# Attention with 32 heads: three independent pairs of probability tiles added by DMA, instead of three tiles added one after another into one sum

## The chip, the cores and the metric

The kernel runs on one core of a Trainium2 chip. The metric is the device time of one execution in microseconds (us). Before the change the median of three runs was 1824.03 us (1816.09, 1824.03, 1825.92).

## What is computed

For 2048 tokens of width 1024 the result is `g * a + (1 - g) * b`: `a` is softmax attention with 32 heads of width 32 and an output projection, `b` a small mixture of experts, `g` a sigmoid gate per token. The change lies in the attention, and there in the sums of the softmax rows:

```python
scores = einsum("bhqd,bhkd->bhqk", q, k) * (Dh ** -0.5)
p = softmax(scores, axis=-1)
o = einsum("bhqk,bhkd->bhqd", p, v)
a = o.transpose(0, 2, 1, 3).reshape(B, S, D) @ wo
```

The kernel takes exp(scores) without dividing, multiplies that with V, and divides by the row sums at the end. So it needs, per head and query, the sum of exp(scores) over the 2048 keys.

## The kernel before

**Tiles and steps.** A head has 16 tiles of 128 keys; its step k makes the tile `P[h, kt]`: 128 keys by 2048 queries, 1 MB in f32. The scores of a tile are four matmuls of 512 queries (L1284) into a ring of seven PSUM banks; ScalarE takes exp of one to four banks at once into the place of P (L1296); TensorE then multiplies P with V (L1308). A list of seven batches per head (L1527) writes the order of TensorE out by hand: 9, 9, 10, 9, 9, 9, 9 score matmuls, and behind those of each batch the products with V of the key tiles that are due (5, 5, 5, 4, 4, 5, 4 halves of a tile; the first five belong to the head before).

**Row sums.** `presum` (L1325) adds the 16 tiles of a head up. Twelve are added by VectorE into `acc` (`add`, L1339: two instructions of 1024 elements). Tile 1 is written by ScalarE straight into a buffer `accd`, and tiles 3, 8 and 12 are added to it by DMA (L1330: `nc.gpsimd.dma_start(ACCD[h], P[h, kt], accum_op=OP.add)`). All three write the same buffer, so each waits until the one before has landed. At step 3 of the next head VectorE adds `accd` to `acc` (`merge4`, L1372, for heads 0 to 23; `merge_even` and `merge_odd` after that; `merge` for the last two). Then DMAs of GpSimd's queue (`fold4`, L1381, and `fold4_end`, L1390) fold `acc` so that four heads (later two) share one tile T, which `head_sums` (L1395) sums over the partitions by matmuls with ones, at step 18 of the head after the fourth. `load_r` and `norm_r` (L1417, L1422) load the sums, take reciprocals and store them.

**Order of work.** Everything that is not a score or a V product is put at a step by `at(step, ...)` (L1470 to L1523), and each engine runs its own instructions in that order. DMAs of SP's queue (K, Q and V of the next head, stores) wait in order behind each other; so do those of GpSimd's queue (POOL in the profile: the accumulations and the folds).

**Places.** `p_tile` (L1158) gives a new tile the place whose planned end `until` is the earliest: 14 steps for a tile that DMA adds, 4 for another. There are 11 places, 9 from the 308th tile on and 8 from the 416th, when three of them (`vhl`, `wo_raw2`, `wo_raw3`) are wanted for weights. The two buffers of `accd` come on top. A place is free in fact when the V product, the addition or the DMA that reads it is done; ScalarE waits for that.

Of the kernel before, what the change touches and what calls it, by code (L numbers as in the profile page):

```python
# [10 lines left out]
F32 = mybir.dt.float32  # L11
# [21 lines left out]
def gated_mha_peer_kernel(ctx, tc, xT, wqkv, wv, wo, wq, k12, ug, v, out):  # L33
# [8 lines left out]
    nc = tc.nc  # L42
# [164 lines left out]
    pairs = [wa.tile([128, 2, 2, HC, 128], F32R, name=f"e{i}") for i in range(2)]  # L207
# [136 lines left out]
    places = {(2, 0): "xh2", (2, 1): "xl1", (3, 0): "xh3", (3, 1): "xl2"}  # L344
# [83 lines left out]
    second = {(0, 0): "A12", (0, 1): "A22", (1, 0): "S3", (1, 1): "S2"}  # L428
# [277 lines left out]
    for blk, (k, n) in enumerate(order):  # L706
        w, c = chunks[k]
        t = pairs[k % 2]
# [378 lines left out]
    def values_unit(u):  # L1087
# [11 lines left out]
        for k, name in enumerate(order):  # L1099
# [6 lines left out]
            if last and name == "P2":  # L1106
                first_scores()
# [39 lines left out]
                for j in {4: (0,), 5: (1,), 6: (2, 3)}.get(k, ()):  # L1147
                    split_early(u - 1, j)

    P, pools, keep = {}, {}, None  # L1150


    SUMS = (1, 3, 8, 12), (2, 4, 6)
    PLACES = (11, 0), (9, 28 * 11), (8, 28 * 11 + 12 * 9)
    LATE = 21, 28
    until = [0] * PLACES[0][0]

    def p_tile(h, kt):  # L1158


        n = [places for places, k in PLACES if pools["next"] >= k][-1]
        pools["next"] += 1
        i = min(range(n), key=lambda i: until[i])
        until[i] = h * NT + kt + (14 if kt in SUMS[h == H - 1] else 4)
        pool, name = ((pools["right"], f"P{i}") if i < 4 else (pools["left"], f"P{i}") if i < 8 else
                      (keep, ("vhl", "wo_raw2", "wo_raw3")[i - 8]))
        P[h, kt] = pool.tile([128, S], F32, name=name)
        return P[h, kt]

    def first_scores():  # L1170

        tp.close()
        pools.update(right=Pool("ppr", side="right"), next=0)
        K, Q = Z
        pt = p_tile(0, 0)
        for qc, i in enumerate((5, 6, 0, 1)):
            ps = ps1.tile([128, 512], F32, name=f"bk{i}")
            c = slice(qc * 512, (qc + 1) * 512)
            nc.tensor.matmul(ps, K[:98, :128], Q[:98, c], start=True, stop=True)
            nc.scalar.activation(pt[:, c], ps, AF.Exp, scale=SCALE)  # L1180
# [23 lines left out]
    keep = Pool("keep")  # L1204
# [4 lines left out]
    rb0 = keep.tile([128, KC, W], F32, name="rb0")  # L1209

    T = rb0.rearrange("p k m -> p (k m)")
# [5 lines left out]
    wk = Pool("wk", bufs=2)  # L1217

    ACC = {0: wk.tile([128, S], F32, name="acc")}
# [3 lines left out]
    pss = Pool("pss", space=PSUM)  # L1223

    KQ = [Z, [kq.tile([128, S], F32R, name=n) for n in ("K1", "Q1")]]
    Vt, O, SM, ACCD, R = {}, {}, {}, {}, {}


    NB = 7
# [41 lines left out]
    def scores(s0, s1):  # L1271


        n = s1 - s0
        banks = ring_banks(n)
        cuts = {c for c in range(1, n + 1) if c == n or (s0 + c) % NQ == 0 or banks[c] == 0}
        cuts |= set(range(1, max(1, n - NB) + 1))
        if n <= 2 * NQ:
            cuts |= {c + 2 for c in range(NQ, n, NQ) if not cuts & {c + 1, c + 3}}
        c0 = 0  # L1280
        for c, i in enumerate(banks):
            (h, kt), qc = divmod((s0 + c) // NQ, NT), (s0 + c) % NQ
            K, Q = KQ[h % 2]
            on_ring(nc.tensor.matmul(ring[:, i, :], K[:98, kt * 128:(kt + 1) * 128],  # L1284
                                     Q[:98, qc * 512:(qc + 1) * 512], start=True, stop=True), i)
            if c + 1 not in cuts:
                continue
            m = c + 1 - c0
            q0 = qc + 1 - m
            if q0 == 0:  # L1290
                if kt == SUMS[h == H - 1][0]:
                    P[h, kt] = ACCD[h] = wk.tile([128, S], F32, name="accd")
                else:
                    p_tile(h, kt)
            i -= m - 1
            on_ring(nc.scalar.activation(  # L1296
                P[h, kt][:, q0 * 512:(q0 + m) * 512].rearrange("p (a m) -> p a m", a=m),
                ring[:, i:i + m, :], AF.Exp, scale=SCALE), *range(i, i + m))
            c0 = c + 1
# [23 lines left out]
                                       start=(src is srcs[0]), stop=(src is srcs[-1]))  # L1323

    def presum(h, kt):  # L1325
        sums = SUMS[h == H - 1]
        if kt == 0 or kt == sums[0] or (h == H - 1 and kt >= NT - 2):
            return
        if kt in sums:
            nc.gpsimd.dma_start(ACCD[h], P[h, kt], accum_op=OP.add)  # L1330
            return
        if kt == 1 + (sums[0] == 1):
            if h > 0:
                ACC[h] = wk.tile([128, S], F32, name="acc")
            add(ACC[h], P[h, 0], P[h, kt])
        else:
            add(ACC[h], ACC[h], P[h, kt])

    def add(out, a, b):  # L1339

        for c in (slice(0, S // 2), slice(S // 2, S)):
            nc.vector.tensor_add(out[:, c], a[:, c], b[:, c])  # L1342

    def merge(h):
        add(ACC[h], ACC[h], ACCD[h])

    up, low = slice(0, 64), slice(64, 128)

    def merge_even(h):
        add(T, ACC.pop(h), ACCD[h])  # L1350

    def fold_even(h):
        nc.gpsimd.dma_start(T[up], T[low], accum_op=OP.add)

    def merge_odd(h):
        add(ACC[h][up], ACC[h][up], ACCD[h][up])
        add(T[low], ACC[h][low], ACCD[h][low])

    def fold_odd(h):
        nc.gpsimd.dma_start(T[low], ACC.pop(h)[up], accum_op=OP.add)  # L1360
# [3 lines left out]
    FOURS = 6  # L1364

    def quarter(i):
        return slice(32 * i, 32 * i + 32)
# [4 lines left out]
    def merge4(h):  # L1372
        q = h % 4
        if q == 0:
            add(T, ACC.pop(h), ACCD[h])
        else:
            mine = quarter(q)
            add(T[mine], ACC[h][mine], ACCD[h][mine])
            add(ACC[h], ACC[h], ACCD[h])

    def fold4(h):  # L1381
        q = h % 4
# [46 lines left out]
    OC, RB = {}, {}  # L1429
# [6 lines left out]

    def load_rb(n, k0, k1, js=range(4), queue=nc.sync):
        if k0 == 0 and js[0] == 0:
            RB[n] = rb0 if n == 0 else wk.tile([128, KC, W], F32, name="accd")
# [30 lines left out]
    def at(step, f, *a):  # L1470
        todo.setdefault(step, []).append((f, a))

    for h in range(H):
        base = h * NT
        g, j = divmod(h, 4)
        if h >= 1 and h + 1 < H:
            at(base - 1, load_head, h + 1)
        if h < H - 1:
            at(base + NT, finish, h)
            if h == H - 2:  # L1480
                at(base + NT + 5, merge, h)
                at(base + NT + 8, head_sums, h)
            elif g < FOURS:
                at(base + NT + 3, merge4, h)
                at(base + NT + 5, fold4, h)
                at(base + NT + 10, fold4_end, h)
            else:
                at(base + NT + 3, (merge_even, merge_odd)[h % 2], h)
                at(base + NT + 5, (fold_even, fold_odd)[h % 2], h)
                if h % 2:  # L1490
                    at(base + NT + 12, head_sums, h - 1, 2)
        if j == 3 and g + 1 < G:
            if g < FOURS:
                at(base + NT + 18, head_sums, h - 3, 4)
            at(base + NT + (22 if g < FOURS else 14), load_r, g)
            at(base + NT + (30 if g < FOURS else 18), norm_r, g)
        if g + 1 < G:
            at(base + 7, load_v, g + 1, j)
    for i, step in enumerate((6, 7, 9, 11)):
# [14 lines left out]
    vhl = []  # L1514
# [7 lines left out]
    at(30 * NT + 13, load_rb, 0, 0, KC - 1, range(2))  # L1522
    at((H - 1) * NT + 2, load_rb, 0, 0, KC - 1, range(2, 4))  # L1523


# [6 lines left out]
    s0, v0, k = NQ, 0, 0  # L1532
    for s1, v1 in batches:
        if s1 > s0:
            scores(s0, s1)
        for part in parts_of(v0, v1):
            pv(*part)
        while NQ * (k + 1) <= s1:
            for f, a in todo.pop(k, []):
                f(*a)  # L1540
            if k < NT * H:
                presum(*divmod(k, NT))
            k += 1
        s0, v0 = s1, v1
# [284 lines left out]
```

## Time and profile before

The profiled execution took 1816.36 us; its span, first to last instruction, is 1814.6 us.

| engine | busy us | share of span | instructions |
|---|---|---|---|
| TensorE (PE) | 1803.1 | 99% | 10631 |
| VectorE (DVE) | 1499.4 | 83% | 1673 |
| ScalarE (ACT) | 1221.6 | 67% | 1615 |
| GpSimd (POOL) | 261.4 | 14% | 314 |

The attention takes the stretch from about 630 to 1635 us. Between 800 and 1000 us TensorE was busy for 200.00 of 200 us, ScalarE for 196.68, VectorE for 188.65, and the 16 DMA engines for 0.95 of the time: four resources are nearly full at once. A busy share there doesn't say which one sets the time; the waits do.

How to read the views: a row of a timeline has the start, the length, engine, line, operation, output<-input and count, and in brackets how long the engine had stood idle and for whom. In a list of waits the numbers are microseconds in total, times, and the longest. `x24` on L1308 are 12 matmuls of the program: an f32 product leaves two records.

### The profile page before, as it was taken

To read this page: it belongs to the slowest core of one execution; us is meant where nothing else is said; L and a number is where in the kernel's file an instruction comes from. 1 tells how busy PE (TensorE), PEld (TensorE's weight loads), DVE (VectorE), ACT (ScalarE), POOL (GpSimd) and SP (SyncE) were. 2 spreads that over 40 slices of the span, in tenths; PEclk is the share of its full clock that TensorE was granted. 3 is DMA by queue.
4 is the path that set the end of the run, shared out by engine and by line. 5 is a ranking of instruction groups with operands and counts; after the bars stand their busy time and mean duration, and the time that the engine had idled before them with its cause. 6 is when DMAs were issued, how large, how long until landed. Compare 5 with 4: busy or idle time off the path is not lost.

```text
span 1814.6 us, 28137 instructions
## 1 busy us (share of the span) xinstructions
PE 1803.1 (99%) x10631; PEld 1137.4 (63%) x10631; DVE 1499.4 (83%) x1673; ACT 1221.6 (67%) x1615; POOL 261.4 (14%) x314
## 2 busy tenths in 40 slices
PE   9999999999999999999999999999999999999999
PEld 7777777788888754455554545554454555547887
DVE  7868785368987789998999998899889999995674
ACT  4434422211243499999999999999998999993221
POOL 0222000026401211111111111111111110101000
PEclk9999999999999999999999999999999999999999
DMA  7788888723248689999999999999998998967851
GB/s 240 235 283 259 265 264 306 252 70 106 82 144 275 228 195 201 192 191 204 196 212 194 213 191 204 184 205 193 184 219 172 204 204 191 207 141 236 272 167 58
DMA packets 132226, 364.74 MB, mean 201 GB/s; under 512 B 17541, under 2 KB 57877, under 8 KB 106169
## 3 DMA queue, kind: packets, MB, share of 16 engines
q0 software_dynamic: 22064, 136.07, 37.9%
q1 hardware_dynamic: 89864, 190.94, 34.7%
q10 hardware_dynamic: 20160, 35.92, 7.0%
q8 instruction: 84, 1.38, 0.3%
q14 instruction: 54, 0.43, 0.1%
HBM read 169.14 MB, written 72.10 MB: 133 GB/s over the span
## 4 chain that ended last, share of the span: by engine, by line
PE 91%; DMA 5%; DVE 2%; issue 1%; ACT 0%; SPq 0%; POOL 0%; ACTq 0%; DVEq 0%; POOLq 0%
PE ring L1284 25%; PE o L1308 22%; PE bk L157 13%; PE bk L713 10%; PE pa L157 6%; PE bk L760 5%; PE pa L1573 2%; PE bk L928 2%; DMA accd<-P 2%; PE bk L313 2%; PE bk L493 1%; DVE acc L1342 1%; DMA rb<-acc 1%; PE pa L1580 1%; PE bk L397 1%
## 5 line engine op out<-in xcount | busy, mean ns | idle before, releaser
L1296 ACT ACTIVATE P<-ring 128x512 f32<-128x512 f32 (+3 forms) x895 | 730.8, 939 | 12.9 <-PE ring L1284 4.9
L1342 DVE TENSOR_TENSOR acc<-acc,P 128x1024 f32<-128x1024 f32 x508 | 583.6, 1217 | 4.9 <-ACT P L1296 4.7
L1308 PE MATMUL o<-P,V 128*32 128x512 f32 (+1 forms) x3624 | 378.0, 531 | 0.0
L1284 PE MATMUL ring<-Q,K 98*128 98x512 f32 x1024 | 270.6, 407 | 3.3 <-ACT P L1296 3.3
L1284 PE MATMUL ring<-z,z 98*128 98x512 f32 x1020 | 267.7, 406 | 0.1
L1284 PEld LDWEIGHTS ring<-Q,K 98*128 98x128 f32 x1024 | 182.8, 188 | 124.6 <-issue 36.6
L1284 PEld LDWEIGHTS ring<-z,z 98*128 98x128 f32 x1020 | 182.1, 188 | 116.2 <-issue 39.9
L1308 PEld LDWEIGHTS o<-P,V 128*32 128x32 f32 x3624 | 100.4, 109 | 191.2 <-issue 171.1
L1330 POOL DMA_DIRECT2D accd<-P x81 | 72.1, 891 | 505.8 <-ACT P L1296 237.4
L1296 ACT ACTIVATE wo_raw<-ring 128x512 f32<-128x512 f32 (+3 forms) x144 | 114.2, 864 | 3.0 <-PE ring L1284 1.6
L1342 DVE TENSOR_TENSOR rb<-acc,accd 32x1024 f32<-32x1024 f32 (+2 forms) x60 | 70.7, 1217 | 54.4 <-DMA accd<-P 29.5
L242 ACT ACTIVATE hi<-bk 128x512 fp32r<-128x512 f32 x40 | 23.7, 595 | 114.2 <-PE bk L713 95.2
L713 PE MATMUL bk<-xh,e 128*128 128x512 f32 x384 | 94.2, 394 | 0.0
L713 PE MATMUL bk<-xl,e 128*128 128x512 f32 x384 | 92.2, 389 | 0.0
L1296 ACT ACTIVATE vhl<-ring 128x512 f32<-128x512 f32 (+3 forms) x106 | 85.5, 872 | 2.1 <-PE ring L1284 0.7
L713 PEld LDWEIGHTS bk<-xh,e 128*128 128x128 f32 x384 | 71.0, 188 | 22.0 <-issue 3.4
L255 DVE TENSOR_TENSOR lo<-bk,hi 128x512 fp32r<-128x512 f32 x40 | 27.5, 689 | 66.8 <-ACT hi L242 61.6
L713 PEld LDWEIGHTS bk<-xl,e 128*128 128x128 f32 x384 | 72.1, 188 | 15.0
L1342 DVE TENSOR_TENSOR acc<-acc,wo_raw 128x1024 f32<-128x1024 f32 x68 | 79.8, 1218 | 0.3 <-ACT wo_raw L1296 0.3
L103 DVE TENSOR_TENSOR e<-wraw,e 128x512 fp32r<-128x512 f32 (+3 forms) x64 | 54.8, 864 | 28.3 <-ACT e L102 27.7
L1342 DVE TENSOR_TENSOR acc<-acc,vhl 128x1024 f32<-128x1024 f32 x62 | 72.9, 1217 | 0.0
L102 ACT ACTIVATE e<-wraw 128x512 fp32r<-128x512 f32 (+3 forms) x64 | 44.7, 705 | 39.1 <-DMA wraw<-in_wqkv 23.4
(305 smaller groups left out, 2550.2 us busy)
## 6 DMA issues: line engine op xcount, KB each, us to landing
accd<-P POOLq DMA_DIRECT2D x81, 1024.0 KB, 11.2
wqt<-in_wq SPq DMA_DIRECT2D x26, 1024.0 KB
wraw<-in_wqkv SPq DMA_DIRECT2D x30, 512.0 KB
rb<-acc POOLq DMA_DIRECT2D x36, 256.0 KB, 7.9
accd<-wo_raw POOLq DMA_DIRECT2D x9, 1024.0 KB, 10.2
qdh<-hi ACTq DMA_DIRECT2D x32, 256.0 KB
qdl<-lo ACTq DMA_DIRECT2D x32, 256.0 KB
kdh<-hi ACTq DMA_DIRECT2D x32, 256.0 KB
```

The lines of the kernel that those rows point to most:

```text
L102: nc.scalar.activation(hi, src, AF.Copy)
L103: (on or nc.vector).tensor_tensor(out=lo, in0=src, in1=hi.bitcast(F32), op=OP.subtract)
L157: nc.tensor.matmul(ps, self.a[a][i][:, k, :], self.b[b][j][k], start=(not first and k == 0 and i == j == 0), stop=(k == HC - 1 and i == 1))
L313: nc.tensor.matmul(ps[32 * quad:32 * quad + 32, :], kpad[:, quad % 2, i, :], t[:, quad, :], start=(i == 0), stop=(i == 3))
L713: nc.tensor.matmul(ps, t[:, kc // HC, a, kc % HC], x_at(b, n, kc), start=first, stop=last)
L760: nc.tensor.matmul(ps, x_at(a, t // 4, kc)[:, tok], b, start=first, stop=last)
L928: nc.tensor.matmul(p, x_at(a, t // 4, kc)[:, tok], b, start=first, stop=last)
L1284: on_ring(nc.tensor.matmul(ring[:, i, :], K[:98, kt * 128:(kt + 1) * 128], Q[:98, qc * 512:(qc + 1) * 512], start=True, stop=True), i)
L1296: on_ring(nc.scalar.activation(P[h, kt][:, q0 * 512:(q0 + m) * 512].rearrange("p (a m) -> p a m", a=m), ring[:, i:i + m, :], AF.Exp, scale ...
L1308: nc.tensor.matmul(O[h][32 * qc:32 * qc + 32, c0:c1], Vt[g][:, kt, 32 * j:32 * j + 32], p[:, qc * 512 + c0:qc * 512 + c1], start=(kt == 0) ...
L1330: nc.gpsimd.dma_start(ACCD[h], P[h, kt], accum_op=OP.add)
L1342: nc.vector.tensor_add(out[:, c], a[:, c], b[:, c])
```

## The change

- **Pairs.** Three pairs of tiles per head, (0, 2), (4, 6) and (8, 10): the DMA adds the second tile to the first, in the first one's place. The pairs have nothing in common. In the last head it is (2, 4) and (2, 6), both into tile 2. The buffer `accd` is gone; every tile is a P tile.
- **When.** The accumulation of a pair is put four steps after its first tile: steps 4, 8 and 12 of its head (in the last head both at 6). It overwrites the first tile, so it waits for the V product of that tile and for exp of both.
- **VectorE.** It adds ten single tiles with nine additions, the first pair at step 12, the second at step 1 of the next head, and the third in the merge at step 5 (before: 3).
- **Folds.** At steps 7 and 11 of the next head (before: 5 and 10); `head_sums` for four heads stays at 18, for two heads goes from 12 to 14.
- **Row sums.** `load_r` from step 22 to 24 and `norm_r` from 30 to 36 (for the later heads 14 to 18, and 18 to 25).
- **Places.** 13, then 11 from head 20, step 8, and 10 from head 27, step 11; two of them (P8, P9) lie where `accd` lay. Planned ends: 14 steps for the first tile of a pair, 10 for the second, 5 for a single one.

```diff
-    SUMS = (1, 3, 8, 12), (2, 4, 6)
-    PLACES = (11, 0), (9, 28 * 11), (8, 28 * 11 + 12 * 9)
+    PAIRS = ((0, 2), (4, 6), (8, 10)), ((2, 4), (2, 6))
+    PLACES = (13, 0), (11, 20 * NT + 8), (10, 27 * NT + 11)
...
-        until[i] = h * NT + kt + (14 if kt in SUMS[h == H - 1] else 4)
+        i = min((i for i in range(n) if i not in (8, 9) or k < H * NT - 8), key=lambda i: until[i])
+        pairs = PAIRS[h == H - 1]
+        until[i] = k + (14 if kt in [b for b, _ in pairs] else 10 if kt in [a for _, a in pairs] else 5)
...
-                if kt == SUMS[h == H - 1][0]:
-                    P[h, kt] = ACCD[h] = wk.tile([128, S], F32, name="accd")
-                else:
-                    p_tile(h, kt)
+                p_tile(h, kt)
...
-        if kt in sums:
-            nc.gpsimd.dma_start(ACCD[h], P[h, kt], accum_op=OP.add)
-            return
-        if kt == 1 + (sums[0] == 1):
+        if kt == second:
             if h > 0:
                 ACC[h] = wk.tile([128, S], F32, name="acc")
-            add(ACC[h], P[h, 0], P[h, kt])
+            add(ACC[h], P[h, first], P[h, kt])
         else:
             add(ACC[h], ACC[h], P[h, kt])
 
+    def accumulate(h, b, a):
+        nc.gpsimd.dma_start(P[h, b], P[h, a], accum_op=OP.add)
+
+    def pair(h, i):
+        return P[h, PAIRS[h == H - 1][i][0]]
+
+    def add_pair(h, i):
+        add(ACC[h], ACC[h], pair(h, i))
...
+        for b, a in PAIRS[h == H - 1]:
+            at(base + b + 4, accumulate, h, b, a)
         if h < H - 1:
+            at(base + 12, add_pair, h, 0)
+            at(base + NT + 1, add_pair, h, 1)
...
             elif g < FOURS:
-                at(base + NT + 3, merge4, h)
-                at(base + NT + 5, fold4, h)
-                at(base + NT + 10, fold4_end, h)
+                at(base + NT + 5, merge4, h)
+                at(base + NT + 7, fold4, h)
+                at(base + NT + 11, fold4_end, h)
...
-            at(base + NT + (22 if g < FOURS else 14), load_r, g)
-            at(base + NT + (30 if g < FOURS else 18), norm_r, g)
+            at(base + NT + (24 if g < FOURS else 18), load_r, g)
+            at(base + NT + (36 if g < FOURS else 25), norm_r, g)
```

More of the change, by code (lines that the diff above doesn't have):

```diff
@@ L1148, in values_unit @@
                     split_early(u - 1, j)
-    P, pools, keep = {}, {}, None
-    SUMS = (1, 3, 8, 12), (2, 4, 6)
-    PLACES = (11, 0), (9, 28 * 11), (8, 28 * 11 + 12 * 9)
+    P, pools, keep, wk = {}, {}, None, None
+    PAIRS = ((0, 2), (4, 6), (8, 10)), ((2, 4), (2, 6))
+    PLACES = (13, 0), (11, 20 * NT + 8), (10, 27 * NT + 11)
     LATE = 21, 28
@@ L1158, in p_tile @@
     def p_tile(h, kt):
-        n = [places for places, k in PLACES if pools["next"] >= k][-1]
-        pools["next"] += 1
-        i = min(range(n), key=lambda i: until[i])
-        until[i] = h * NT + kt + (14 if kt in SUMS[h == H - 1] else 4)
+        k = h * NT + kt
+        n = [places for places, k0 in PLACES if k >= k0][-1]
+        i = min((i for i in range(n) if i not in (8, 9) or k < H * NT - 8), key=lambda i: until[i])
+        pairs = PAIRS[h == H - 1]
+        until[i] = k + (14 if kt in [b for b, _ in pairs] else 10 if kt in [a for _, a in pairs] else 5)
         pool, name = ((pools["right"], f"P{i}") if i < 4 else (pools["left"], f"P{i}") if i < 8 else
-                      (keep, ("vhl", "wo_raw2", "wo_raw3")[i - 8]))
-        P[h, kt] = pool.tile([128, S], F32, name=name)
+                      (wk, f"P{i}") if i < 10 else (keep, ("vhl", "wo_raw2", "wo_raw3")[i - 10]))
+        P[h, kt] = pool.tile([128, S], F32, name=name, bufs=1)
         return P[h, kt]
@@ L1172, in first_scores @@
         tp.close()
-        pools.update(right=Pool("ppr", side="right"), next=0)
+        pools.update(right=Pool("ppr", side="right"))
         K, Q = Z
@@ L1225, in gated_mha_peer_kernel @@
     KQ = [Z, [kq.tile([128, S], F32R, name=n) for n in ("K1", "Q1")]]
-    Vt, O, SM, ACCD, R = {}, {}, {}, {}, {}
+    Vt, O, SM, R = {}, {}, {}, {}
     NB = 7
@@ L1325, in presum @@
     def presum(h, kt):
-        sums = SUMS[h == H - 1]
-        if kt == 0 or kt == sums[0] or (h == H - 1 and kt >= NT - 2):
+        pairs = PAIRS[h == H - 1]
+        first, second = [t for t in range(NT) if t not in sum(pairs, ())][:2]
+        if kt in sum(pairs, ()) or kt == first or (h == H - 1 and kt >= NT - 2):
             return
-        if kt in sums:
-            nc.gpsimd.dma_start(ACCD[h], P[h, kt], accum_op=OP.add)
-            return
-        if kt == 1 + (sums[0] == 1):
+        if kt == second:
             if h > 0:
                 ACC[h] = wk.tile([128, S], F32, name="acc")
-            add(ACC[h], P[h, 0], P[h, kt])
+            add(ACC[h], P[h, first], P[h, kt])
         else:
             add(ACC[h], ACC[h], P[h, kt])
+    def accumulate(h, b, a):
[4 more added lines that the diff above has]
+        add(ACC[h], ACC[h], pair(h, i))
     def add(out, a, b):
@@ L1344, in merge @@
     def merge(h):
-        add(ACC[h], ACC[h], ACCD[h])
+        add_pair(h, -1)
     up, low = slice(0, 64), slice(64, 128)
     def merge_even(h):
-        add(T, ACC.pop(h), ACCD[h])
+        add(T, ACC.pop(h), pair(h, -1))
     def fold_even(h):
@@ L1355, in merge_odd @@
     def merge_odd(h):
-        add(ACC[h][up], ACC[h][up], ACCD[h][up])
-        add(T[low], ACC[h][low], ACCD[h][low])
+        add(ACC[h][up], ACC[h][up], pair(h, -1)[up])
+        add(T[low], ACC[h][low], pair(h, -1)[low])
     def fold_odd(h):
@@ L1374, in merge4 @@
         if q == 0:
-            add(T, ACC.pop(h), ACCD[h])
+            add(T, ACC.pop(h), pair(h, -1))
         else:
             mine = quarter(q)
-            add(T[mine], ACC[h][mine], ACCD[h][mine])
-            add(ACC[h], ACC[h], ACCD[h])
+            add(T[mine], ACC[h][mine], pair(h, -1)[mine])
+            add_pair(h, -1)
     def fold4(h):
@@ L1438, in load_rb @@
         if k0 == 0 and js[0] == 0:
-            RB[n] = rb0 if n == 0 else wk.tile([128, KC, W], F32, name="accd")
+            RB[n] = rb0 if n == 0 else wk.tile([128, KC, W], F32, name=f"P{8 + n % 2}", bufs=1)
         for j in js:
@@ L1483, in gated_mha_peer_kernel @@
             elif g < FOURS:
-                at(base + NT + 3, merge4, h)
-                at(base + NT + 5, fold4, h)
-                at(base + NT + 10, fold4_end, h)
-            else:
-                at(base + NT + 3, (merge_even, merge_odd)[h % 2], h)
-                at(base + NT + 5, (fold_even, fold_odd)[h % 2], h)
+                at(base + NT + 5, merge4, h)
+                at(base + NT + 7, fold4, h)
+                at(base + NT + 11, fold4_end, h)
+            else:
+                at(base + NT + 5, (merge_even, merge_odd)[h % 2], h)
+                at(base + NT + 7, (fold_even, fold_odd)[h % 2], h)
                 if h % 2:
-                    at(base + NT + 12, head_sums, h - 1, 2)
+                    at(base + NT + 14, head_sums, h - 1, 2)
         if j == 3 and g + 1 < G:
@@ L1521, in gated_mha_peer_kernel @@
     at((H - 1) * NT + 3, load_o, 0, 2, KC - 1)
-    at(30 * NT + 13, load_rb, 0, 0, KC - 1, range(2))
+    at(30 * NT + 15, load_rb, 0, 0, KC - 1, range(2))
     at((H - 1) * NT + 2, load_rb, 0, 0, KC - 1, range(2, 4))
```

## The prediction

> **What bounds the kernel now.** I read the page first, then the stretches head by head, then the waits inside the attention. The page says that TensorE has no room:
>
> ```profile
> span 1814.6 us, 28137 instructions
> PE 1803.1 (99%) x10631; PEld 1137.4 (63%) x10631; DVE 1499.4 (83%) x1673; ACT 1221.6 (67%) x1615; POOL 261.4 (14%) x314
> ```
>
> A head's end is marked by one copy of its output on ScalarE (L1405). Two such marks, one head apart, and stretches cut at marks (columns: stretch, length, PE, PEld, DVE, ACT, POOL busy, granted clock, DMA share, GB/s):
>
> ```profile
> 1128.07 0.67 ACT L1405 ACTIVATE osb<-o 128x512 f32<-128x512 f32 x1
> 1159.02 0.67 ACT L1405 ACTIVATE osb<-o 128x512 f32<-128x512 f32 x1
> ```
>
> ```profile
> 691.46:1252.95 561.49, 561.49 (x3921) 282.65 (x3922) 523.14 (x464) 551.48 (x697) 87.15 (x104) 1.00 0.95 199
> 1284.16:1317.25 33.09, 32.26 (x225) 15.75 (x224) 28.23 (x26) 31.01 (x43) 5.15 (x6) 1.00 0.91 191
> 1348.25:1384.35 36.10, 32.81 (x217) 15.92 (x218) 29.93 (x28) 30.59 (x38) 5.94 (x7) 0.95 0.91 185
> 1384.35:1604.97 220.62, 220.62 (x1545) 110.57 (x1546) 208.50 (x186) 215.48 (x273) 25.64 (x30) 1.00 0.90 197
> 1372.00:1374.00 2.00, 2.00 (x13) 0.45 (x16) 2.00 (x3) 2.00 (x3) 0.00 (x0) 0.50 0.98 102
> ```
>
> An undisturbed head is 30.95 us (1159.02 - 1128.07). The first stretch is 18 heads with four `head_sums` of about 0.95: (561.49 - 3.8) / 18 = 30.98, so nothing is lost there. The head of 33.09 has a `head_sums` and lost 33.09 - 31.9 = 1.2 us; the head of 36.10 has none and lost 5.1. The last stretch is 7 heads with four: 7 x 30.97 + 3.8 = 220.6, no loss. The head between the first two stretches (31.21) lost 0.2. Together **6.5 us is all that waiting cost TensorE** in this execution. The rest is its own work, which the change leaves alone. The largest loss in the chain of waits (start, length, what; the first row is wanted further down):
>
> ```profile
> 1279.03 10.29 DMA rb<-acc
> ...
> 1350.06 12.19 DMA accd<-P
> ...
> 1362.35 2.36 DVE rb L1342 x2
> 1364.73 4.64 DVE acc L1342 x4
> ...
> 1369.45 1.03 ACT P L1296
> ...
> 1370.53 1.77 PE ring L1284 x4
> ```
>
> The third accumulation of a head, issued at 1350.06, lands at 1362.3; the merge on VectorE waited for it, the additions behind the merge came late, ScalarE got its place of P late, TensorE its bank. TensorE stood 3.3 us, and afterwards ran two microseconds at a clock of 0.50 (row above), which makes 5.1. The other waits of this sort stay hidden, but are many (who waited for L1330, and its landings):
>
> ```profile
>   DVE rb L1342: 48.1, 17
> DMA to landing us min/median/max: 6.9/11.2/15.7
> ```
>
> Seventeen merges waited 48.1 us for a landing. Why so late shows in one head on the queue of GpSimd, and VectorE at its end:
>
> ```profile
> 1132.70 0.86 POOL L1330 DMA_DIRECT2D accd<-P  x1 [4.60 <-PE o L1308]
> 1143.90 0.78 POOL L1387 DMA_DIRECT2D acc<-acc  x1 [10.34 <-DVE acc L1342]
> 1144.42 1.06 POOL L1388 DMA_DIRECT2D rb<-acc  x1
> 1145.86 0.90 POOL L1330 DMA_DIRECT2D accd<-P  x1 [0.39 <-ACT vhl L1296]
> 1152.93 0.78 POOL L1393 DMA_DIRECT2D rb<-acc  x1 [6.17 <-DMA rb<-acc]
> 1160.39 0.90 POOL L1330 DMA_DIRECT2D accd<-wo_raw  x1 [6.68 <-ACT P L1296]
> ```
>
> ```profile
> 1172.31 2.36 DVE L1342 TENSOR_TENSOR rb<-acc,accd 128x1024 f32<-128x1024 f32 x2 [3.72 <-DMA accd<-wo_raw]
> ```
>
> This head's scores began at about 1123.5 (mark 1128.07 less the first batch, 4.57, below). Tile 3's accumulation goes out 9.2 us into it, tile 8's behind a fold at 22.4, tile 12's, which must await the landing of tile 8's, at 36.9, though its tile is ready near 24.6. It lands 11.9 us later, 3.7 too late.
>
> **The change, part by part.** The clock of a head comes from TensorE and VectorE:
>
> ```profile
> 1190.89 2.28 PE ring L1284 x9
> 1193.17 2.29 PE o L1308 x24
> ```
>
> ```profile
> 1238.63 13.71 DVE L1342 TENSOR_TENSOR acc<-acc,P 128x1024 f32<-128x1024 f32 x12
> ```
>
> Nine scores are 2.28 us (0.253 each), x24 are five halves of a tile (0.46 each), an addition is 13.71 / 6 = 2.28. With the seven batches (9, 9, 10, 9, 9, 9, 9 scores; halves 5, 5, 5, 4, 4, 5, 4 in the order of time, the first five of the head before) they end at 4.57, 9.1, 14.0, 18.1, 22.2, 26.8 and 30.9 us, which agrees with 30.95; a step is 1.93.
>
> *Work.* Accumulations stay at 31 x 3 + 2 = 95. VectorE: before, 12 tiles with 11 additions and a merge; after, 10 tiles with 9, two pairs and a merge: again 11 and the merge. ScalarE, TensorE and the bytes are the same. So no engine gains or loses work, zero; what changes is when.
>
> *When a pair starts.* Needed are the V product of its first tile and exp of its second: tile 0's product ends at 9.1 - 1.37 = 7.8 us, tile 4's at 14.0, tile 8's at 22.2; the exps of 2, 6 and 10 are earlier. On GpSimd's queue the order is (0, 2), fold of the head before, (4, 6), end of the fold, (8, 10). The fold waits for the merge, which ends at 15.4 (next paragraph), so (4, 6) goes out at about 15.5 + 1.9 = 17.4 (1.96 us from 1143.90 to 1145.86). The fold's end waits for the fold's landing, 7.9 us by the page:
>
> ```profile
> rb<-acc POOLq DMA_DIRECT2D x36, 256.0 KB, 7.9
> ```
>
> That is 23.4, and (8, 10) follows at 24.3.
>
> *When it is needed.* VectorE gets tile 11 at 23.4 (two of its scores lie in the sixth batch, plus an exp) and then has no pause: tile 11 until 25.7, pair one to 28.0, tiles 12 to 15 to 37.1, pair two to 39.4, tiles 1 and 3 of the next head to 41.7, the merge of two additions to 46.4, which is 15.4 in that head; tiles 5, 7, 9 to 22.3, 1.1 us before tile 11. So the landings may take 25.7 - 7.8 = **17.9 us**, 37.1 - 17.4 = **19.7** and 41.7 - 24.3 = **17.4**. They took 11.2 in the middle and 15.7 at most. The 48.1 us of waits on VectorE go, and with them the losses of TensorE, **-6.5 us**. What is late next is VectorE's own run from step 11 to 21 without a pause.
>
> *Places.* The plan holds (3 x 14 + 3 x 10 + 10 x 5) / 16 = 7.6 places; 5.4, 3.4 and 2.4 of 13, 11 and 10 are spare. Against the times above, tile 0 is free 0.5 steps after its planned end (28.0 us is step 14.5), tile 8 2.0 (46.4 is 24.0), tile 4 2.4 (39.4 is 20.4, planned 18); all others keep theirs. Left are 3.0 steps (5.8 us), 1.0 (1.9 us) and none. So from head 20 on, and above all in the last four, ScalarE may wait for a place now and then. No row shows such a wait in a kernel with pairs; the bounds are 0 and what the old waits cost, 6.5. I take **+2 us**, half a microsecond in each of the last four heads, nearer to 0, since a late landing no longer adds to it.
>
> *Two accumulations in flight.* Unknown too. Each took 6.9 to 15.7 us with at most a fold and loads beside it; between 6.9 and 2 x 11.2 = 22.4 I take 11.2, since here (4, 6) starts 9.6 us after (0, 2) and (8, 10) 6.9 after (4, 6): they overlap little. The Trainium skill, "DMA: Bandwidth & Descriptors", section "Issuing engines are not separate DMA queues", says that DMAs from all engines run on the same 16 engines and interleave; by that rule independence buys no bandwidth, and the sum would end at the third rival's figure if the 11.2 us were all transfer. The trace has folds beside accumulations, as the rule says, but no row with the price.
>
> *The rest.* `head_sums` at the unchanged step 18: the fold's end goes out at 23.5, and such an end took 10.3 us in the chain above (1279.03), that is 33.8, or 2.9 us in the next head; TensorE comes there at 9.1. Cost 0, cover 6.2 us. `norm_r` later: VectorE has the same two small instructions; SP no longer stands for them ahead of the next head's K and Q, which costs nothing now as those are a head ahead. In the last head VectorE ends one addition later, 2.3 us; the row sums there begin at 1639.51, and the additions ended at 1636.2 (rows below), so between 0 and 1 us; I take 0.
>
> ```profile
> 1639.51 1.04 PE L1321 MATMUL o<-acc,ones 128*32 128x512 f32 x8
> ```
>
> ```profile
> 1633.94 2.35 DVE L1342 TENSOR_TENSOR acc<-acc,P 128x1024 f32<-128x1024 f32 x2
> ```
>
> **Sum.** Profiled execution 1816.36 - 6.5 + 2 = 1811.9. That execution is near the fastest of the runs shown (1816.09); the other two are 8 and 10 us above it. The one thing in the trace that varies by so much and reaches TensorE is the landing (6.9 to 15.7), so I take their excess for more of the same waits, which go as well. Forecast: **1812 us**, 0.66% under the median of 1824.03. Below 1809.9 nothing can be gained, as that is TensorE's own work.
>
> **Rivals.**
> 1. *Little is gained.* The spread from 1816 to 1826 has another cause, outside the attention, or new short waits take the old ones' place. For it: only 6.5 us of loss are shown, and no view shows the slower runs. Against it: 17 late merges. The floor of 1810 plus 8 to 10 gives 1818 to 1820; with it all 1815 to 1824.
> 2. *Waits for places.* With margins of 1.9 us and none, VectorE needs to be only 1 to 2 us later than worked out. Eleven heads (21 to 31) with 1 to 2 us each: 1810 + 11 to 22, some 1821 to 1832, say 1826. Against it: VectorE's 1.1 us per head of spare catches up.
> 3. *Slower: transfers share.* Two in flight on full DMA engines (share 0.95, above) slow each other. It decides from a landing of 17.4 + 1.1 = 18.5 us on: from there each further microsecond is lost per head where places are short. At 22.4: 22.4 - 18.5 = 3.9 us in 11 heads, 1810 + 43, about 1853. Against it: 6.9 us as the shortest landing, so 11.2 is in good part waiting for others; and the folds already ran beside accumulations. The rule of the Trainium skill's DMA page, quoted above, speaks for this rival.
> 4. *It does not do what it says:* the pairs queue behind the folds on GpSimd and so keep a chain through the merge. The queue holds them 3.4 and 2.1 us in the sums above, and the merge does not wait for the last of them unless that landing exceeds 17.4; then the result is rival 1's, 1815 to 1824.
>
> **Chances.** Forecast 0.62 (1809 to 1814.9), rival 1 0.19, rival 4 0.05, rival 2 0.06, rival 3 0.08. A measurement of this kernel can tell 0.5% from no change: below 1814.9 is faster, above 1833.1 slower. Faster 0.62, same 0.30 (rivals 1, 2 and 4), slower 0.08. The range from 1808.5 to 1824 holds the forecast and rivals 1 and 4, 0.86.
>
> **What would show it.** VectorE waiting for accumulations under 5 us in all (48.1 now); accumulations about 8, 17 and 24 us into a head, landing in under 17; heads of 30.95 throughout, also 23; waits of ScalarE for VectorE only from head 20 on and under 3 us in all. Wrong would be: landings with a median over 17 (rival 3), heads after 20 all above 31.5 (rival 2), or a TensorE as full as forecast with a total still near 1820 (rival 1).

## The result, and the profile after

The changed kernel takes **1810.99 us**, the median of six runs (1810.27 to 1811.52), against 1824.62 (1816.09 to 1828.13) of the kernel before in the same six rounds: a ratio of 0.9933, 95% interval 0.9911 to 0.9956. The forecast was 1812. Not only the median moved: the runs of before lie 12 us apart, those of after 1.3. Part of the gain is luck in these six runs of before: over 31 later ones, with ten of after beside them (last row of the table of parts), the medians are 1818.58 and 1811.07, 7.5 us apart and not 13.6.

The profiled execution took 1811.52 us, 4.84 less than that of before. From the page of after:

```profile
span 1809.7 us, 28079 instructions
...
PE 1801.0 (100%) x10631; PEld 1137.0 (63%) x10631; DVE 1503.6 (83%) x1673; ACT 1221.5 (67%) x1613; POOL 262.4 (15%) x314
...
PE 97%; DMA 2%; ACT 0%; issue 0%; DVE 0%; SPq 0%; ACTq 0%; DVEq 0%
```

The last row is the chain that ended last. TensorE holds 97% of it; it was 91% before, with 5% for DMA and 2% for VectorE. The same four stretches as in the prediction, cut at this kernel's marks:

```profile
692.29:1253.66 561.37, 561.37 (x3921) 282.56 (x3922) 531.33 (x469) 551.30 (x696) 87.92 (x104) 1.00 0.99 198
1284.62:1316.59 31.97, 31.97 (x225) 15.95 (x226) 27.57 (x25) 31.05 (x43) 4.25 (x5) 1.00 1.01 217
1347.55:1378.49 30.94, 30.94 (x217) 15.63 (x218) 30.11 (x28) 30.50 (x38) 5.06 (x6) 1.00 1.03 205
1378.49:1599.04 220.55, 220.55 (x1545) 110.69 (x1546) 204.50 (x181) 215.72 (x271) 25.75 (x30) 1.00 0.91 195
```

The second column (length) and the third (TensorE busy) agree in every row, and the granted clock is 1.00: TensorE waits for nothing in them. The head that took 33.09 us before takes 31.97, the one of 36.10 takes 30.94. The landings, and who waited for an accumulation:

```profile
  DVE rb L1347: 1.4, 2
...
DMA to landing us min/median/max: 6.9/12.0/15.4
```

48.1 us of waits have become 1.4, though a landing takes about as long as before (11.2 in the middle there, 15.7 at most). The DMAs got no faster; they start earlier. GpSimd's queue over the head whose scores begin at 1124.2 (mark 1128.76 less 4.57):

```profile
1132.57 0.86 POOL L1336 DMA_DIRECT2D P<-P  x1 [11.58 <-PE o L1306]
1140.35 0.78 POOL L1392 DMA_DIRECT2D acc<-acc  x1 [6.91 <-DVE acc L1347]
1140.86 1.06 POOL L1393 DMA_DIRECT2D rb<-acc  x1
1141.36 1.48 POOL L1336 DMA_DIRECT2D P<-P  x1
1149.61 0.78 POOL L1398 DMA_DIRECT2D rb<-acc  x1 [6.77 <-DMA rb<-acc]
1150.13 1.19 POOL L1336 DMA_DIRECT2D P<-P  x1
```

The three pairs (L1336) go out 8.4, 17.2 and 25.9 us into the head. Before it was 9.2, 22.4 and 36.9. They stand in the worked-out order: the second behind a fold, the third behind its end.

**Where the 4.84 us come from.** From the first head's mark to the last the attention took 974.46 us before and 967.67 after, 6.79 less. The rest of the kernel took 841.90 (1816.36 - 974.46) and takes 843.85, 1.95 more. Part of that is seen behind the last head:

```profile
1635.30 10.06 DMA smd<-ssb
...
1645.41 1.69 DMA rr<-smd
...
1653.93 11.19 PE pa L1582 x48
```

In this chain the store of the last head's row sums took 10.06 us to land, the load of them could only follow, and TensorE stood 0.95 us ahead of 1653.93. Most of the rest lies ahead of the attention: the first head's mark is at 660.46 before and at 661.30 after, 0.84 later. In the profiles of this document it lies anywhere from 660.08 to 662.76, with pairs and without, so this part isn't put down to the change.

### The profile page after: what moved, and what is told of

The parts are those of the page before. It is cut to its first block, busy times and chain, and to the rows that moved or that the text cites. A ratio compares the mean times of both kernels' runs of the same rounds, so it can differ in the third digit from the quotient of the medians.

```text
span 1809.7 us, 28079 instructions
## 1 busy us (share of the span) xinstructions
PE 1801.0 (100%) x10631; PEld 1137.0 (63%) x10631; DVE 1503.6 (83%) x1673; ACT 1221.5 (67%) x1613; POOL 262.4 (15%) x314
## 4 chain that ended last, share of the span: by engine, by line
PE 97%; DMA 2%; ACT 0%; issue 0%; DVE 0%; SPq 0%; ACTq 0%; DVEq 0%
PE ring L1285 29%; PE o L1306 26%; PE bk L157 13%; PE bk L713 10%; PE pa L157 6%; PE bk L760 5%; PE bk L928 2%; PE bk L313 2%; PE pa L1582 2%; PE bk L493 1%; PE bk L397 1%; PE pa L1589 1%; DMA wraw<-in_wqkv 1%; DMA smd<-ssb 1%; PE ring L1319 0%; ACT P L1294 0%
## 5 line engine op out<-in xcount | busy, mean ns | idle before, releaser
L1294 ACT ACTIVATE P<-ring 128x512 f32<-128x512 f32 (+3 forms) x995 | 807.8, 932 | 12.9 <-PE ring L1285 6.7
L1347 DVE TENSOR_TENSOR acc<-acc,P 128x1024 f32<-128x1024 f32 x516 | 596.0, 1219 | 30.5 <-ACT P L1294 29.8
L1306 PE MATMUL o<-P,V 128*32 128x512 f32 (+1 forms) x3896 | 408.7, 540 | 0.0
L1306 PEld LDWEIGHTS o<-P,V 128*32 128x32 f32 x3896 | 108.4, 109 | 203.8 <-issue 179.7
L1336 POOL DMA_DIRECT2D P<-P x78 | 81.4, 1043 | 496.5 <-PE o L1306 190.5
L1347 DVE TENSOR_TENSOR acc<-acc,wo_raw 128x1024 f32<-128x1024 f32 x118 | 139.0, 1220 | 13.4 <-ACT wo_raw L1294 13.4
L1294 ACT ACTIVATE wo_raw<-ring 128x512 f32<-128x512 f32 (+3 forms) x134 | 119.6, 988 | 0.0
L713 PE MATMUL bk<-xh,e 128*128 128x512 f32 x384 | 94.2, 394 | 0.0
L1347 DVE TENSOR_TENSOR acc<-P,P 128x1024 f32<-128x1024 f32 x60 | 70.8, 1221 | 16.2 <-ACT P L1294 15.9
L157 PE MATMUL bk<-xh,e 128*128 128x512 f32 x288 | 68.5, 393 | 0.0
L1306 PE MATMUL o<-wo_raw,V 128*32 128x256 f32 (+1 forms) x632 | 66.6, 496 | 0.0
```

The lines of the kernel that those rows point to most:

```text
L157: nc.tensor.matmul(ps, self.a[a][i][:, k, :], self.b[b][j][k], start=(not first and k == 0 and i == j == 0), stop=(k == HC - 1 and i == 1))
L713: nc.tensor.matmul(ps, t[:, kc // HC, a, kc % HC], x_at(b, n, kc), start=first, stop=last)
L1294: on_ring(nc.scalar.activation(P[h, kt][:, q0 * 512:(q0 + m) * 512].rearrange("p (a m) -> p a m", a=m), ring[:, i:i + m, :], AF.Exp, scale ...
L1306: nc.tensor.matmul(O[h][32 * qc:32 * qc + 32, c0:c1], Vt[g][:, kt, 32 * j:32 * j + 32], p[:, qc * 512 + c0:qc * 512 + c1], start=(kt == 0) ...
L1336: nc.gpsimd.dma_start(P[h, b], P[h, a], accum_op=OP.add)
```

## Experiments

**Theory 1**, the prediction's: the accumulations of a head waited for one another's landing, and the pairs don't; the places are tight. **Theory 2**: it is the steps. Merge and folds two steps later (M), or the load and reciprocal of the row sums later (N), are enough without pairs (P; the letters stand for these parts below). **Theory 3**: the long runs of before come from outside the attention. Each timed kernel below has ten runs (four for the four pairs), and the kernel before ran beside them: 74 runs with medians of 1818.58 to 1819.63 in three groups, lowest 1810.27, highest 1830.94.

**Before again, twice.** No edit; a look at longer executions.

> The kernel before, unchanged, profiled again to meet one of its longer executions. Prediction: whatever it takes over 1810 us is TensorE waiting in the attention behind late landings: an execution of 1820 to 1828 shows 10 to 18 us lost in heads, with VectorE waiting 60 us or more for accumulations. Rival: the heads lose 6 us as in the first profile and the rest lies before or behind the attention.

> The same kernel once more, for a second execution: its time over 1810 us is again the sum of what its heads lose; rival: a loss outside the attention.

They took 1819.12 and 1817.97 us. The attention took 976.78 and 975.98, 9.1 and 8.3 more than in after (967.67); the rest 842.34 and 841.99, as in the shortest (841.90). So the excess lies in the attention, against theory 3 (no execution near the longest, 1830.94, was profiled). The chain of waits in the first:

```profile
1117.66 15.96 DMA accd<-P
...
1134.16 11.64 DMA accd<-P
...
1145.89 2.37 DVE rb L1342 x2
1148.28 3.56 DVE acc L1342 x4
```

and the queue of GpSimd behind it:

```profile
1150.94 0.78 POOL L1387 DMA_DIRECT2D acc<-acc  x1 [14.98 <-DVE acc L1342]
1151.45 1.06 POOL L1388 DMA_DIRECT2D rb<-acc  x1
1151.95 1.48 POOL L1330 DMA_DIRECT2D accd<-P  x1
1160.08 0.78 POOL L1393 DMA_DIRECT2D rb<-acc  x1 [6.65 <-DMA rb<-acc]
```

This is a **loop**. A second accumulation (1117.66) lands late, the third (1134.16) must await it, the merge (1145.89) awaits the third, the fold (1150.94) awaits the merge, and the next head's second accumulation stands behind the fold on the queue (1151.95). Round once: 34.3 us (1117.66 to 1151.95), where a head has 31; in the second execution 33.6. A head that begins it late hands on more lateness, until TensorE stands. The long landing at 1117.66 is part of it: with two landings of 11.0 us, the middle in this profile, I estimate the round at 34.3 - 15.96 - 11.64 + 22.0 = 28.7 us, and lateness would shrink: by this estimate it takes long landings to feed the loop. TensorE's two stalls:

```profile
1154.51 1.18 PE L1284 MATMUL ring<-z,z 98*128 98x512 f32 x4 [2.08 <-ACT wo_raw L1296]
...
1171.26 1.07 PE L1321 MATMUL ring<-rb,ones 128*32 128x512 f32 x8 [2.31 <-DVE acc L1342]
```

The first stall goes by a place of P, as the prediction had it. The second is `head_sums`, which needs the fold's end, issued at 1160.08; the bracket names VectorE, but that had long been done, and the time fits the DMA's landing. The prediction counted such a loss, 1.2 us in the head of 33.09, without asking for its way.

**Serial.** In the changed kernel each accumulation is made to wait for the landing of the pair before, by four bytes read from it. Places, steps and bytes stay.

```diff
     def accumulate(h, b, a):
+        i = PAIRS[h == H - 1].index((b, a))
+        if i and h < H - 1:
+            nc.gpsimd.dma_start(MARK[h:h + 1, i:i + 1], pair(h, i - 1)[0:1, 0:1])
         nc.gpsimd.dma_start(P[h, b], P[h, a], accum_op=OP.add)
```

> Pairs, steps and places of the changed kernel; but ahead of the second and third accumulation of a head stands a DMA of 4 bytes that reads the sum just written, so the queue waits until the one before has landed (the whole result is still computed). Theory of the chain (independence is what helped): accumulations go out about 8, 21 and 33 us into a head instead of 8, 17 and 26, the third lands near 45 where it is wanted at 41.7; VectorE waits some 3 us per head for landings, 60 to 100 us in all, of which it can make up 1.1 per head; the time goes to 1830 to 1860. Rival (later steps and more places did it): within 2 us of the changed kernel, 1810 to 1813.

1817.33 us (1813.02 to 1826.79), ratio to before 0.9993 (0.9964 to 1.0021). The dependence costs 6 us against after (1810.99), most of the gain or all of it, and brings the spread back; both figures expected were missed. Its profile is that of its fastest run (1813.02). There the third accumulation and the merge that needs it:

```profile
1156.76 0.93 POOL L1340 DMA_DIRECT2D P<-P  x1
```

```profile
1169.15 2.36 DVE L1351 TENSOR_TENSOR rb<-acc,P 128x1024 f32<-128x1024 f32 x2 [2.60 <-DMA P<-P]
```

32.6 us into the head instead of 25.9, and a merge 2.6 us late, as worked out. But all such waits together, 15 of them, are 24.7 us, 2.7 at most, and the attention took 968.63 us, only 1.0 more than in after. So this profile shows the dependence making accumulations and merges late; where the median loses 6 us, no profile shows, and the 62 issues that the edit adds to GpSimd's queue were not tested apart from the waiting.

**Steps only.** The kernel before, with its three accumulations into one `accd`, and M and N.

```diff
-                at(base + NT + 3, merge4, h)
-                at(base + NT + 5, fold4, h)
-                at(base + NT + 10, fold4_end, h)
+                at(base + NT + 5, merge4, h)
+                at(base + NT + 7, fold4, h)
+                at(base + NT + 11, fold4_end, h)
...
-            at(base + NT + (30 if g < FOURS else 18), norm_r, g)
+            at(base + NT + (36 if g < FOURS else 25), norm_r, g)
```

> The kernel before with the later steps alone: merge at 5, folds at 7 and 11, head sums of two at 14, the row sums' load and reciprocal later; still three tiles in sequence into one sum, and its own places. Theory of the chain: the merge asks 2.3 us later, but the fold ahead of the second accumulation on GpSimd's queue is later too, so VectorE still waits 15 to 40 us for landings and the time is 1813 to 1822. Rival (the later merge did it): under 5 us of waits and 1810 to 1812.

1810.18 us (1809.09 to 1818.43; nine of ten under 1813.1), ratio 0.9959 (0.9934 to 0.9985). Theory 1 said that this leaves most of the loss; it falls as the only cause. The same head in this kernel's profile, one of its fastest runs (1809.25):

```profile
1132.51 0.86 POOL L1330 DMA_DIRECT2D accd<-P  x1 [9.63 <-PE o L1308]
1140.23 0.78 POOL L1387 DMA_DIRECT2D acc<-acc  x1 [6.86 <-DVE acc L1342]
1140.74 1.06 POOL L1388 DMA_DIRECT2D rb<-acc  x1
1143.12 0.90 POOL L1330 DMA_DIRECT2D accd<-P  x1 [1.32 <-ACT P L1296]
1148.98 0.78 POOL L1393 DMA_DIRECT2D rb<-acc  x1 [4.96 <-DMA rb<-acc]
1154.00 0.90 POOL L1330 DMA_DIRECT2D accd<-wo_raw  x1 [4.24 <-ACT P L1296]
```

The fold, put two steps *later*, goes out *earlier* (1140.23; in the kernel before 1143.90), since its merge no longer waits. The second accumulation follows at 1143.12, with 1.32 us of idle queue between: it no longer stands behind the fold. The third still goes out 10.9 us after the second, a landing's time (10.8 in the middle there), but that is 1154.00 and not 1160.39. So the accumulations still wait for one another and the loop is broken all the same, at the fold. Merges waited 9.3 us in all, between the two figures expected, and no head is long.

**The parts one by one.** Pairs and places (P) with the old steps; P with the later load and reciprocal (N); and, without pairs, M alone and N alone. Each is the edits shown above, taken apart; in M alone, load and reciprocal of the last groups stand at 16 and 20, behind their `head_sums`.

> The changed kernel with the old steps: merge at 3, folds at 5 and 10, head sums of two at 12, row sums' load and reciprocal as before; pairs and places are the new ones. Theory of the chain: landings may still take 17.9, 15 and 17 us where 12 are taken, so VectorE waits under 5 us in all, and 1810 to 1812. Rival (the later steps are needed): VectorE waits over 15 us for landings, 1813 or more.

> The kernel before with only the merge two steps later (5) and the folds behind it (7 and 11; head sums of two at 14, and only for the one group of late heads that needs it load and reciprocal 2 steps later); three tiles in one sum. Theory of the loop (late landing, late merge, late fold on GpSimd's queue, late next accumulation, which goes round in 32 to 34 us where a head has 30.95): the merge has 2.3 us more, the loop does not start, VectorE waits under 20 us for accumulations and no head before the last ones is longer; 1809 to 1813. Rival (the later reciprocal made the difference in the kernel with all later steps): 1815 to 1824.

> The kernel before with only the row sums' load and reciprocal later (24 and 36, late heads 18 and 25). Theory of the loop: nothing in the loop changes, VectorE waits 40 to 65 us for accumulations, 1816 to 1824. Rival (these waits for the reciprocal's load set the loop off): under 20 us of waits, 1809 to 1813.

> The changed kernel with the merge back at step 3 and the folds at 5 and 10, but the later load and reciprocal kept. The kernel with pairs and all old steps lost 3.9 us in one head, behind a reciprocal that waited 8.3 us for its load. If that was all it lost: no head longer than 30.95 (31.95 with head sums), 1810 to 1812, and a spread of its runs under 3 us. If pairs need the later merge: VectorE waits over 10 us for accumulations and single heads are longer, 1812 or more.

> The changed kernel unchanged, beside the others on the same chip: 1810 to 1812, spread under 2 us, no head longer. If the later steps alone are as good as the whole change, the kernel with them alone (1810.2 in the middle) is not slower than this one by more than 1 us.

| kernel | median us | lowest to highest | ratio to before (95%) | merges' waits in its profile, us |
|---|---|---|---|---|
| before | 1818.58 to 1819.63 | 1810.27 to 1830.94 | | 48.1, 53.7, 58.0 |
| M | 1818.70 | 1809.71 to 1822.26 | 0.9991 (0.9967 to 1.0016) | 17.8 |
| N | 1810.98 | 1809.70 to 1819.33 | 0.9971 (0.9949 to 0.9994) | 41.7 |
| M and N | 1810.18 | 1809.09 to 1818.43 | 0.9959 (0.9934 to 0.9985) | 9.3 |
| P | 1812.62 | 1810.65 to 1816.93 | 0.9960 (0.9939 to 0.9982) | 7.6 |
| P and N | 1811.23 | 1810.53 to 1812.07 | 0.9965 (0.9947 to 0.9984) | 0.8 |
| P, M and N (after) | 1811.07 | 1809.99 to 1813.82 | 0.9963 (0.9949 to 0.9978) | 0.9 |

The waits of a row come from one profile, so from one run: a fast one for M (1809.71) and for M and N, a long one for N (1815.08) and for P (1815.19). Pairs alone bring the median down by 7.0 us (1819.63 to 1812.62, beside each other), and so does N alone, by 7.6 (1818.58 to 1810.98; by the ratio in the table it is 5, between 1 and 9). Together they bring no more. M by itself moves no median. Only with pairs *and* N is none of ten runs above 1814. The intervals of all versions with P or N overlap: none beats the changed kernel with certainty, and its own worst run is 4.6 us under that of M and N (which ran on another chip, as did P).

Here the theory of the loop failed twice. It expected 1809 to 1813 us of M, which moves a merge and a fold of the loop, and got 1818.70; of N, which leaves the loop alone, it expected 1816 to 1824 and got 1810.98. N's rival failed too: it wanted under 20 us of merges' waits, and there were 41.7. Nor did N's own profile lose the loop. It went round in 34.2 us (from the first row below to the next second accumulation at 1150.03), and two heads took 32.80 and 34.68 us:

```profile
1115.85 15.70 DMA accd<-P
...
1132.10 11.78 DMA accd<-P
...
1143.97 2.37 DVE rb L1342 x2
```

So the loop is there in the profiled long runs of before and of N, but what makes the runs of a kernel short or long is not settled by it.

One thing that N moves out of the way is seen in the profile of P alone. There one head took 34.90 us, and this is its chain:

```profile
1042.31 19.51 DMA smd<-ssb
...
1061.96 9.34 DMA rr<-smd
...
1071.39 0.56 DVE rr L1429
...
1079.11 0.61 ACT P L1294
```

The store of the row sums, 8 KB, took 19.51 us to land, its load 9.34 more, and VectorE stood 8.33 us for it at the reciprocal, with the additions behind it. ScalarE then lacked a place and TensorE stood 2.0 us. With N the reciprocal comes six steps later. In the three profiles of before this wait is 1.5 us at most, so by which way N helps there is open. And M alone was profiled in its fastest run (no long head), so what makes six of its ten runs 1818 or longer is open too. P, M and N beside them spread over 3.8 us, where under 2 was expected.

**Eleven places.** The changed kernel with two places fewer throughout.

```diff
-    PLACES = (13, 0), (11, 20 * NT + 8), (10, 27 * NT + 11)
+    PLACES = (11, 0), (9, 20 * NT + 8), (8, 27 * NT + 11)
```

> The changed kernel without the two more places: 11, 9 and 8 instead of 13, 11 and 10, all else alike. By the working of the prediction 5.4, 3.4 and 2.4 spare places become 3.4, 1.4 and 0.4, and a first tile of a pair is freed 2.4 steps after its planned end: 1 step left in the first 20 heads, 1 to 2 short in the last 11. Then ScalarE waits 2 to 4 us per head there, and the time is 1830 to 1855. Rival (places were never short, since the changed kernel shows no wait for one even with 10): 1810 to 1813.

1816.97 us (1814.56 to 1818.87), ratio 0.9984 (0.9962 to 1.0006), between the two figures expected. Marks of the last heads:

```profile
1472.89 0.67 ACT L1410 ACTIVATE osb<-o 128x512 f32<-128x512 f32 x1
1503.89 0.62 ACT L1410 ACTIVATE osb<-o 128x512 f32<-128x512 f32 x1
1538.53 0.66 ACT L1410 ACTIVATE osb<-o 128x512 f32<-128x512 f32 x1
1573.32 0.60 ACT L1410 ACTIVATE osb<-o 128x512 f32<-128x512 f32 x1 [0.18 <-PE o L1306]
1606.82 0.67 ACT L1410 ACTIVATE osb<-o 128x512 f32<-128x512 f32 x1
```

The head up to 1503.89, with nine places, takes 31.00; those with eight 34.64, 34.79 and 33.50, where after took 31.85, 30.97 and 31.89. Nine cost nothing, eight some 2 to 4 us a head; in the head of 34.79 the reciprocal had also stood 4.53 us for its load. The changed kernel has at least ten.

**A late third pair.** (12, 14) instead of (8, 10), which leaves its landing 11.7 us rather than 17.4.

```diff
-    PAIRS = ((0, 2), (4, 6), (8, 10)), ((2, 4), (2, 6))
+    PAIRS = ((0, 2), (4, 6), (12, 14)), ((2, 4), (2, 6))
```

> The changed kernel with pairs (0, 2), (4, 6), (12, 14) instead of (8, 10) as the third; all else alike. Tile 12's product ends at 30.0 us of the head, the merge wants the sum near 41.7: 11.7 us are left where landings took 12.0 in the middle and 15.4 at most. Theory of the chain (a landing later than VectorE asks is what costs): VectorE waits 0 to 3.5 us in most merges, 20 to 60 us in all; its 1.1 us of spare per head makes up part, and the time is 1812 to 1825. Rival (waits on VectorE for landings are hidden anyway and independence alone decides): 1810 to 1812 whatever the allowance.

1818.98 us (1813.60 to 1823.71), ratio 1.0003 (0.9981 to 1.0025), inside the range that the theory expected: the whole gain is gone. Who waited, and the landings:

```profile
  DVE rb L1347: 42.9, 24
...
DMA to landing us min/median/max: 6.9/12.4/15.6
```

24 merges wait again, with landings as in after. But most of these waits cost nothing: heads 1 to 19, with 13 places, and 21 to 27, with 11, are as long as in after. The attention took 9.4 us more than there. Head 20, in which the places go down to 11, lost 1.6 of them (32.56 us), and heads 28 to 30, with ten, the rest (33.46, 36.17 and 32.78). In the longest VectorE and TensorE stood so:

```profile
1562.97 0.55 DVE L1429 RECIPROCAL rr<-rr 128x64 f32<-128x64 f32 x1 [7.95 <-DMA rr<-smd]
```

```profile
1574.89 3.14 PE L1285 MATMUL ring<-z,z 98*128 98x512 f32 x7 [4.15 <-ACT P L1294]
```

That is the reciprocal's wait for its load again, in spite of N, and 5.2 us of the 9.4 lie in its head. So independence without time for the landing brought nothing in the median, and the late landings are seen; but that they cost the whole of it is not shown. They were seen to cost only in head 20 and where there are ten places, and there a slow load of the row sums costs as well.

**Four pairs.** (12, 14) as well, so 4 MB a head by DMA and one addition less on VectorE.

```diff
-    PAIRS = ((0, 2), (4, 6), (8, 10)), ((2, 4), (2, 6))
+    PAIRS = ((0, 2), (4, 6), (8, 10), (12, 14)), ((2, 4), (2, 6))
+            at(base + NT + 4, add_pair, h, 2)
```

> The changed kernel with a fourth pair (12, 14) per head: 4 MB instead of 3 by accumulation, VectorE one addition per head less. It asks how much room the DMA engines have, whose busy share is already 1.0 in most of the attention. If the share means that they are full: a third more accumulation does not fit into 30.95 us, landings grow beyond 18 us, VectorE waits in every head, and the time is 1850 to 2000. If a good part of the share is packets waiting for each other: landings of 12 to 16 us, and with VectorE relieved by 2.3 us per head 1810 to 1820.

1940.88 us, ratio 1.0656 (1.0625 to 1.0686), with most heads at 31 to 44 us and one at 58.92:

```profile
  DVE acc L1347: 99.3, 34
  DVE rb L1347: 79.3, 26
...
DMA to landing us min/median/max: 6.8/16.8/23.2
```

Now a landing takes 16.8 us in the middle (with the same late pair in place of the third it was 12.4): what rival 3 feared, one accumulation further on. The Trainium skill, "DMA: Bandwidth & Descriptors", section "Issuing engines are not separate DMA queues", says that all DMAs share the same 16 engines. The traces fit that: the landings grow with a fourth accumulation, and the share of DMA time is 0.94 between 800 and 1200 us before, 1.00 after, 0.98 here with longer heads. Three accumulations a head with their folds fit here, four don't.

## Why the prediction was right, and where not

- **Floor, 1809.9.** Right to within a microsecond: the lowest runs of the seven rows in the table of parts lie between 1809.09 and 1810.65.
- **-6.5 us of waits.** Right: -6.79 in the attention, and VectorE's waits 1.4 us, under the 5 named.
- **When pairs start.** 7.8, 17.4 and 24.3 us worked out, 8.4, 17.2 and 25.9 measured; the third is 1.6 late, as the fold ahead of it went out 0.65 us later than worked out and took 8.75 us to land (1140.86 to 1149.61) in place of 7.9. All three stay within what their landings may take; with the late third pair, beyond that limit, merges waited 42.9 us.
- **Two in flight.** 11.2 us taken, 12.0 measured. The four pairs show how near the other end was.
- **+2 us for places.** Mis-sized: 0 with ten places, and 0 with nine. The plan of steps was at least one place too pessimistic.
- **Behind the last head, 0.** Mis-sized: TensorE stood 0.95 us, inside the bound of 0 to 1, but by the landing of a store and not by VectorE's late addition, which the prediction had in mind. With the 0.84 us ahead of the first head this makes up for the 2 us of places, so that the sum (1811.9) came near the 1811.5 measured by luck, by errors of opposite sign.
- **"I take their excess for more of the same waits".** Right as far as seen: in two longer executions, 3 and 2 us above the first, the excess lay in the attention, and the loop was there. But M, with few such waits in its profile, kept the long runs.
- **"`norm_r` later ... costs nothing now".** The step that failed. The prediction put the worth of the later load and reciprocal at nothing, and N alone moves the median by 7.6 us. It looked at SP's queue, and not at VectorE, which stood 8.33 us for the load in P alone, when the store was slow. Whether that wait is what N takes from the kernel before is not shown.
- **Independence as the cause.** Half right. Making the pairs wait again costs 6.3 us (serial, 1817.33 against 1811.07, not beside each other), and pairs alone give 7.0; but later steps on the old accumulations do as much. The prediction saw each late landing as its own; that a late merge makes the *next* head's accumulation late, through a fold on an in-order queue, it showed in its rows (1143.90, 1145.86) and did not follow round.

## What to carry to other kernels

Follow a late transfer round the loop, through whatever stands behind it on an in-order queue, into the next iteration, and compare the round with the iteration's length: if it is longer, lateness grows. That such a loop is seen does not yet make it the cause: here the part that moves its merge and fold (M) moved no median, and a part outside it (N) did. Where the runs of a kernel spread and its profile is of a short one, the gain is in the spread, and one profile shows too little of it. Test each part of a change alone, the ones costed at nothing too.

## What the runs showed of the hardware

Small transfers can be late too. An 8 KB store took 10.06 us to land in after, with a DMA share of 0.83 over the time, and 19.51 in P alone, with 0.95; there no accumulation of 1 MB took more than 16.6.

A short stall of TensorE can slow what follows. In the kernel with eleven places it stood 1.97 us ahead of 1564.72, and 1.25 ahead of 1597.92; these are stretches behind them (granted clock is the third figure from the end):

```profile
1566.00:1569.00 3.00, 3.00 (x18) 1.27 (x11) 3.00 (x4) 2.00 (x3) 0.00 (x0) 0.50 0.93 219
1598.00:1600.00 2.00, 2.00 (x17) 1.19 (x21) 2.00 (x3) 2.00 (x3) 0.00 (x0) 1.00 0.37 74
```

After 1.97 us the clock was halved for some three microseconds (and so it was after 2.01 in P alone), after 1.25 it was not. The Trainium skill, "TensorE: Matmul & The Clock Gate", section "What's actually happening", has the half clock after an idle window of about 3.4 us. The measurement differs: here 2 us were enough.
